# Squared-ReLU attention with a gated convolution: seven uneven query chunks a batch, or six of four tiles with the 25th tile's product turned round

## The chip, the cores and the metric

The kernel runs on one core of a Trainium2 chip. The metric is the device time of one execution in microseconds (us); three runs of the kernel before gave 2265.54 to 2267.61 us, median 2266.53. Engines are named as in the profile: PE is TensorE (matmuls) and PEld its loading of weights, DVE is VectorE, ACT is ScalarE, POOL is GpSimd, SP issues most DMAs.

## What is computed

```python
scores = scale * np.matmul(z, z.transpose(0, 2, 1))      # scale = 1/S; z is (8, 3200, 64)
attn = np.maximum(scores, 0.0) ** 2
x = u * np.matmul(attn, v)                                # u, v are (8, 3200, 256)
xp = np.concatenate([np.zeros((B, K - 1, D)), x], axis=1)
gate_pre += conv_w[k][None, None, :] * xp[:, k:k + S, :]  # for k in range(5)
gate = 1.0 / (1.0 + np.exp(-gate_pre))
out = (gate * (x @ w_val)) @ w_out                        # both weights are (256, 256)
```

Everything is float32. All products are made of three: each operand is split into a high part (float32r) and a low part (the rest), and high by high, high by low and low by high are added up in PSUM.

## The kernel before, in words

A batch has 3,200 positions, which are 25 tiles of 128. The queries of a batch are cut into seven chunks of 4, 4, 4, 4, 3, 3 and 3 tiles (the last batch: 4, 4, 4, 4, 4, 3, 2). For each chunk the keys are passed over in 13 steps, twelve pairs of tiles and the single last one, so a batch has 91 steps. In a step TensorE makes the scores of two key tiles against the chunk's queries (`scores`, into one of two PSUM bank pairs `s`), ScalarE applies ReLU and square (L581, L582) and casts the high part `ah` (L584), VectorE subtracts for the low part `al` (L590), and TensorE adds the product with v into the two banks `acc` (one for each half of the 256 features): v is stationary and the weights of the attention move, up to 512 columns wide. The scores are made three steps ahead of their product (`AHEAD`).

The matrix of scores is symmetric. A block that an earlier chunk has computed is transposed by VectorE (`turned`, L460 and L470), written to DRAM (`mir`) and later fetched (`m`), three steps ahead of its cast (`FETCH`); for such a step TensorE makes no scores.

Matmuls come in two forms. `side_by_side` (L386) splits the 128 rows of the contraction in two halves of 64 and issues matmuls of the two halves in turn, to two banks: a pair. Steps that have neither scores nor other work in them run as `attend_whole` (L634), 128 rows at once.

A chunk's conv stage runs beside the next chunk's steps, by the table `BEHIND`: x (u times attention, L664), its high and low part (L686, L691), five taps of the convolution for each half of the features (L703, L705), the sigmoid (L710), the product with `w_val` into the banks `misc`, its product with the gate (`gv`, L763, one for each of the two banks, at steps 6 to 9) and that one's high and low part (L767, L772). The product with `w_out` (`project`) goes into the same `misc` banks in the chunk after that, and its result through `ob` to DRAM. The order on each engine is the order in which the code issues the instructions: the loop over the steps issues TensorE's work of a step (attention products, scores, and what fills it), then what the table `todo` holds for the step, then the casts of the weights. Loads of z and v for the next batch, their transposes and their high and low parts have tables of their own (`Z_FROM`, `V_LOAD`, `V_HIGH`). At the end the last chunk's conv stage has nothing beside it; ten matmuls without use (`no_wait`, L393) stand in it.

In the code, `b` is the batch, `c` the chunk, `i` the pair of key tiles, `h` and `e` halves of the features, `P` is 128, `DH` is 2, `D` is 256, `CW` is 512 columns.

## Time and profile before

| what | value |
| --- | --- |
| time, median of three runs | 2266.53 us |
| span of the profiled execution | 2267.0 us |
| TensorE busy | 2259.1 us, 21,193 matmuls |
| VectorE busy | 1850.3 us, 2,421 instructions |
| ScalarE busy | 1746.5 us, 2,314 instructions |
| GpSimd busy | 67.8 us, 110 instructions |
| DMA | 380.73 MB, mean 168 GB/s |

The profile is of one execution, with a page of summaries and a trace behind it. In a group's row stand the line of the code, the engine, the operation, output and input, the shape and the count; then the busy time in us and the mean of one instruction in ns; then the idle time of the engine ahead of these instructions and whose work ended it. In the timeline a row has its start, its length, engine, line and operation. Matmuls are pipelined: the length of one is longer than the interval at which they start, so intervals are read from starts. A busy time of a group is the union of its matmuls' lengths.

### The profile page before, as it was taken

How to read it: one execution, taken by the hardware profiler on the slowest of the kernel's cores; microseconds unless marked ns; L12 is line 12 of the kernel's file. 1: busy time of each engine (PE TensorE's matmuls, PEld its weight loads, DVE VectorE, ACT ScalarE, POOL GpSimd, SP SyncE). 2: the span in 40 equal slices, each digit the busy share in tenths (PEclk: the TensorE clock that was granted, in tenths of full speed). 3: DMA queues.
4: the chain of work that ended last, by engine and by line, in shares of the span. 5: the costliest groups of instructions: out<-in, count | busy, mean ns of one | idle time of the engine just before them, and what ended most of it. 6: DMA issues, size and time to landing. Idle time of an engine off the chain costs nothing.

```text
span 2267.0 us, 52349 instructions
## 1 busy us (share of the span) xinstructions
PE 2259.1 (100%) x21193; PEld 1989.1 (88%) x21193; DVE 1850.3 (82%) x2421; ACT 1746.5 (77%) x2314; POOL 67.8 (3%) x110
## 2 busy tenths in 40 slices
PE   9999999999999999999999999999999999999999
PEld 7889988899888998889988899888998889988888
DVE  8887798877888779887888877888788887888776
ACT  8986799766987659877698776987769876697755
POOL 0000000000000000000000000000000000000000
PEclk9999999999999999999999999999999999999999
DMA  5555867779677786777877868778697776877753
GB/s 120 118 135 133 198 161 161 177 164 211 164 161 175 168 202 162 164 180 169 199 160 170 182 160 195 160 177 182 152 205 164 181 172 161 195 168 175 195 149 93
DMA packets 696547, 380.73 MB, mean 168 GB/s; under 512 B 399600, under 2 KB 666864, under 8 KB 696304
## 3 DMA queue, kind: packets, MB, share of 16 engines
q1 hardware_dynamic: 695104, 377.11, 71.7%
q8 instruction: 166, 2.72, 0.5%
q14 instruction: 77, 0.63, 0.1%
q10 hardware_dynamic: 1200, 0.26, 0.1%
HBM read 208.74 MB, written 168.49 MB: 166 GB/s over the span
## 4 chain that ended last, share of the span: by engine, by line
PE 99%; DVE 1%; issue 0%; ACT 0%; DVEq 0%
PE acc L386 68%; PE s L386 11%; PE misc L386 10%; PE acc L634 8%; PE misc L826 1%; PE misc L750 1%; PE misc L393 0%; DVE x L664 0%; DVE turned L470 0%; DVE v_hl L373 0%; DVE ah L586 0%; PE acc L826 0%; PE s L750 0%; DVE zhl L236 0%; DVE a L519 0%
## 5 line engine op out<-in xcount | busy, mean ns | idle before, releaser
L386 PE MATMUL acc<-ah,v_hl 64*128 64x512 f32 (+1 forms) x9800 | 1530.7, 369 | 1.8 <-DVE x L664 1.1
L386 PEld LDWEIGHTS acc<-ah,v_hl 64*128 64x128 f32 x9800 | 910.7, 184 | 135.2 <-DVE x L664 1.9
L386 PE MATMUL acc<-al,v_hl 64*128 64x512 f32 (+1 forms) x4900 | 911.5, 369 | 0.0
L590 DVE TENSOR_TENSOR al<-a,ah 128x1024 fp32r<-128x1024 f32 (+3 forms) x380 | 414.9, 1092 | 215.3 <-ACT ah L584 208.3
L386 PEld LDWEIGHTS acc<-al,v_hl 64*128 64x128 f32 x4900 | 459.4, 184 | 65.8 <-DVE al L508 0.9
L581 ACT ACTIVATE a<-s 128x1024 f32<-128x1024 f32 (+3 forms) x380 | 348.9, 918 | 169.8 <-PE s L386 158.7
L582 ACT ACTIVATE a<-a 128x1024 f32<-128x1024 f32 (+3 forms) x380 | 364.3, 959 | 12.1
L584 ACT CAST ah<-m 128x768 fp32r<-128x768 f32 (+2 forms) x309 | 275.0, 894 | 128.0 <-DMA m<-mir 53.1
L590 DVE TENSOR_TENSOR al<-m,ah 128x768 fp32r<-128x768 f32 (+2 forms) x309 | 314.8, 1020 | 40.5 <-ACT ah L584 38.9
L584 ACT CAST ah<-a 128x1024 fp32r<-128x1024 f32 (+3 forms) x345 | 328.6, 952 | 11.3
L460 DVE STREAM_TRANSPOSE turned<-a 128x1024 f32<-128x1024 f32 (+2 forms) x324 | 326.0, 1013 | 2.2 <-DMA mir<-turned 1.6
L705 DVE SCALAR_TENSOR_TENSOR gate<-x,cw,gate 128x512 f32<-128x512 f32 (+2 forms) x448 | 304.4, 679 | 4.4 <-ACT gate L703 0.3
L386 PE MATMUL s<-zq,zhl 64*128 64x512 f32 (+3 forms) x1722 | 230.2, 371 | 0.0
L386 PEld LDWEIGHTS s<-zq,zhl 64*128 64x128 f32 x1722 | 157.6, 184 | 26.1
L634 PE MATMUL acc<-ah,v_hl 128*128 128x384 f32 (+2 forms) x700 | 177.6, 331 | 0.2 <-DVE x L664 0.2
L664 DVE TENSOR_TENSOR x<-acc,ut 128x512 f32<-128x512 f32 (+2 forms) x112 | 65.8, 629 | 82.4 <-PE acc L386 53.4
L634 PEld LDWEIGHTS acc<-ah,v_hl 128*128 128x128 f32 x700 | 124.6, 188 | 4.7 <-issue 1.9
L634 PE MATMUL acc<-al,v_hl 128*128 128x384 f32 (+2 forms) x350 | 115.4, 330 | 0.0
L710 ACT ACTIVATE gate<-gate 128x512 f32<-128x512 f32 (+2 forms) x112 | 65.5, 585 | 60.6 <-DVE gate L705 60.4
L767 ACT CAST gvh<-gv 128x512 fp32r<-128x512 f32 (+2 forms) x112 | 64.0, 572 | 44.3 <-DVE gv L763 44.1
L763 DVE TENSOR_TENSOR gv<-misc,gate 128x512 f32<-128x512 f32 (+1 forms) x110 | 69.7, 633 | 17.2 <-PE misc L386 10.7
L703 ACT ACTIVATE gate<-x,cw 128x512 f32<-128x512 f32 (+2 forms) x111 | 75.0, 676 | 2.6 <-DVE x L664 2.6
(133 smaller groups left out, 1954.9 us busy)
## 6 DMA issues: line engine op xcount, KB each, us to landing
m<-mir SPq DMA_DIRECT2D x193, 384.0 KB, 5.1
mir<-turned SPq DMA_DIRECT2D x344, 192.0 KB, 3.3
mir<-turned SPq DMA_DIRECT2D x196, 256.0 KB, 4.0
m<-mir SPq DMA_DIRECT2D x98, 512.0 KB, 5.0
u_raw<-in_u_dram SPq DMA_DIRECT2D x264, 64.0 KB, 3.7
v_raw<-in_v_dram SPq DMA_DIRECT2D x116, 128.0 KB, 4.7
mir<-turned SPq DMA_DIRECT2D x84, 144.0 KB, 2.6
out_dram<-ob SPq DMA_DIRECT2D x92, 128.0 KB, 3.0
```

Of the source, the lines that this page charges most:

```text
L386: ins = nc.tensor.matmul(out_, st[r], mv[r], start=first, stop=last)
L460: nc.vector.transpose(into[:, t : t + m], a[:, j * w : (j + m) * w].rearrange("p (t m x) -> p t m x", t=m, x=BLK))
L581: nc.scalar.activation(a.rearrange("p (j x) -> p j x", j=2), s[:, :, :each], AF.Relu, scale=scale)
L582: nc.scalar.activation(a, a, AF.Square)
L584: nc.scalar.copy(hi, a)
L590: nc.vector.tensor_tensor(lo, a, f32(hi), op=ALU.subtract)
L634: nc.tensor.matmul(out_, st, mv, start=first, stop=last)
L664: nc.vector.tensor_tensor(x[:, h, HALO : HALO + w], accs[b, c][h][:, :w], ut[b, c][:, h, :w], op=ALU.mult)
L703: (first or nc.scalar.mul)(g, tap, cw[:, h, 0:1])
L705: nc.vector.scalar_tensor_tensor(g, tap, cw[:, h, k : k + 1], g, op0=ALU.mult, op1=ALU.add)
L710: nc.scalar.activation(g, g, AF.Sigmoid)
L763: nc.vector.tensor_tensor(gv[:, :w], pvs[b, c][e][:, :w], gates[b, c][:, e, :w], op=ALU.mult)
```

## The change

There are now six chunks of four tiles. The 25th tile of the queries has no chunk: its attention product is made in steps of the sixth chunk, written out as strings (`LAST_MIX`, `FIRST_MIX`): K is the step of the single key tile, whose scores for the 25th tile are made with those of the sixth chunk; O, F and C are the chunk's own, fetched and computed steps; each of three S steps takes eight key tiles of the 25th tile, whose scores were all computed by earlier chunks and are fetched. A batch has 81 steps.

In these products the attention weights are stationary (128 queries wide) and v moves: its two halves side by side, high and low part in 512 columns, then the high part in 256 (`swap_list`). The two halves of the rows go to the two banks of one of the two bank pairs `s`, which stays taken (`held_s`) until `one_take`: ScalarE copies one bank, VectorE adds the other to it and then the two halves of the result. In the meantime scores use the other bank pair alone.

The result has queries on the partitions, not features. The 25th tiles of two batches go together (`GROUPS`; the last two batches each alone): u is multiplied in by GpSimd, TensorE transposes (`one_turn`), and the group has a conv stage of its own (`one_place` to `one_out`), its steps counted from the start of the batch after the group: transposes at step 22 (the tenth step, numbered 9, of the second chunk, numbered 1), value product at 35 and 36, output product at 48 and 49.

Attention steps outside the last eight steps of the program are all pairs now. The loads of z and v and their parts have moved: those of z for the next batch start from the middle of the batch before on (`Z_FROM` counts from the next batch's start). The end of the program is new: after the last chunk's steps come the last 24 key tiles of the 25th tile's product, whole, and then the conv stages of the last chunk and of the last group; the ten matmuls without use are gone.

```diff
-    n_chunks = -(-NT // 4)
-    base, extra = divmod(NT, n_chunks)
-    even = [base + 1] * extra + [base] * (n_chunks - extra)
...
+    assert NT % 4 == 1
+    n_chunks = NT // 4
+    ONE = n_chunks
+    sizes = [4] * n_chunks + [1]
+    firsts = [4 * c for c in range(n_chunks + 1)]
...
+    LAST_MIX = {False: "KFOFFSFFFSFOSFFF", True: "FFOFFFFFOKFFFSSS"}
+    FIRST_MIX = "KCOFFSCFFSFOSFFF"
...
+    def s_bank():
+        if held_s[0] is None:
+            next_s[0] = 1 - next_s[0]
+            x = 1 - next_s[0]
+        else:
+            x = 1 - held_s[0]
+        return ps.tile([P, 2, 512], F32, name=f"s{x}", bufs=1)
...
+    def swap_list(b, c, i, bank):
+        if b not in swaps:
+            held_s[0] = next_s[0]
+            swaps[b] = ps.tile([P, 2, 512], F32, name=f"s{held_s[0]}", bufs=1)
+            swapped[b] = 0
+        out_ = swaps[b][:, bank]
+        if c == ONE:
+            k, n = tiles(c, i)
+            ah, al = (x[:, : n * P].rearrange("p (j x) -> p j x", j=n) for x in at[b, c, i])
+        else:
+            k, n, w = NT - 1, 1, sizes[c] * P
+            ah, al = (x[:, w : w + P].rearrange("p (j x) -> p j x", j=1) for x in at[b, c, i])
+        mms = []
+        for j in range(n):
+            both_v = vt[b, (k + j) // 2][:, :, (k + j) % 2]
+            first = swapped[b] + j == 0
+            last = swapped[b] + j == NT - 1
+            whole = (out_.rearrange("p (x d) -> p x d", x=2), ah[:, j], both_v, first, last)
+            half = (out_[:, :D], al[:, j], both_v[:, 0], False, False)
+            mms += [whole, half] if first else [half, whole]
+        return mms
+    def swap(b, c, i, piece=0, pieces=1):
+        sides = [swap_list(b, c, i, bank) for bank in range(2)]
+        side_by_side(*cut(sides, piece, pieces))
+        if piece == pieces - 1:
+            swapped[b] += tiles(c, i)[1]
...
+    GROUPS = ((0, 1), (2, 3), (4, 5), (6,), (7,))
...
+    def one_take(b, halves=True):
+        g, t = group_of(b)
+        if t == 0:
+            one_sum[g] = sb.tile([P, 2, D], F32, name="one_sum", bufs=1)
+        banks = swaps.pop(b)
+        part = sb.tile([P, CW], F32, name="gv", bufs=1)
+        if halves:
+            nc.scalar.copy(part, banks[:, 1])
+            nc.vector.tensor_tensor(part, banks[:, 0], part, op=ALU.add)
+            nc.vector.tensor_tensor(one_sum[g][:, t], part[:, :D], part[:, D:], op=ALU.add)
...
+        next_s[0] = held_s[0]
+        held_s[0] = None
...
+                for x in range(2):
+                    to = one_turned[g][x][:, (t * DH + h) * half : (t * DH + h + 1) * half]
+                    src = one_sum[g][rows[x], t, h * P : (h + 1) * P]
+                    nc.tensor.matmul(to, src, ident1[rows[x]], start=True, stop=True, is_transpose=True)
...
-    Z_FROM = {b: (-12, -7, -1, 7, 17, 23, 37) if b > 1 else (22, 26, 4, 8, 15, 30, 37) for b in range(1, B)}
-
-    U_LOAD = ((6, -1, -8, -11, -11, -11, -6), (-6, -2, -2, -9, -11, -11, -7))
-    U_PREP = ((11, 2, 1, 2) + (1,) * (n_chunks - 4), (10, 10, 3) + (1,) * (n_chunks - 3))
+    Z_FROM = {b: (-53, -48, -41, -33, -22, -10, -15) if b > 1 else (-17, -13, -35, -31, -24, -9, -5) for b in range(1, B)}
...
+    V_HIGH = (7, 8, 9, 10, 12, 13, 14, 15, 18, 19, 16, 17, 4)
...
+            if steps[s][1] == ONE and s < WHOLE_FROM:
+                for piece in range(2):
+                    fill_at(s + piece, swap, *steps[s], piece, 2)
+                done = s + 1
+            elif both(*steps[s][1:]) and s < WHOLE_FROM:
+                fill_at(s, swap, *steps[s])
+        if b < B - 1:
+            at_step(done, one_take, b)
...
+    for g, members in enumerate(GROUPS[:-1]):
+        s0 = start(members[-1] + 1, 0)
+        at_step(s0 + 6, one_load, g)
+        at_step(s0 + 9, one_mul, g)
+        fill_at(s0 + 22, one_turn, g)
+        at_step(s0 + 22, one_place, g)
+        at_step(s0 + 23, one_high, g)
+        at_step(s0 + 24, one_low, g)
+        for h in range(DH):
+            for k in range(KW):
+                at_step(s0 + 24 + 4 * h + max(k - 1, 0), one_conv, g, h, k)
+        at_step(s0 + 32, one_sigmoid, g)
+        for part in range(2):
+            fill_at(s0 + 35 + part, one_value, g, part)
+        for e in range(DH):
+            at_step(s0 + 36 + e, one_gated, g, e)
+        at_step(s0 + 37, one_gated_high, g)
+        at_step(s0 + 38, one_gated_low, g)
+        for part in range(2):
+            fill_at(s0 + 48 + part, one_project, g, part)
+        at_step(s0 + 49, one_out, g)
...
-            if not halved:
-                assert not left
-                if before:
-                    project_whole(*before)
-                for h in range(DH if 0 <= s < END else 0):
-                    attend_whole(b, c, i, h)
...
+            if s >= WHOLE_FROM:
+                assert not left and not terms and not piece and not before
+                if s < END:
+                    for h in range(DH):
+                        attend_whole(b, c, i, h)
+                    if both(c, i):
+                        swap_whole(b, c, i)
...
+        for h in range(DH):
+            attend_whole(*steps[END], h)
+        project_whole(b, c - 1)
...
+        for s in range(END + 1, N):
+            swap_whole(*steps[s])
+        for x in range(DH):
+            out_copy(b, c - 1, x)
+        out_store(b, c - 1)
+        for k in range(1, KW):
+            conv(b, c, 1, k)
+        sigmoid(b, c, one[0])
+        sigmoid(b, c, one[1])
+        one_take(b, False)
+        one_mul(g, nc.vector)
...
         for e in range(DH):
             value_whole(b, c, e, spare=True)
-        no_wait(*warm, 10)
+        one_turn(g)
+        one_place(g)
...
+        for h in range(DH):
+            for k in range(KW):
+                one_conv(g, h, k)
+        one_sigmoid(g)
+        project_whole(b, c, spare=True)
+        for part in range(2):
+            one_value(g, part)
+        for e in range(DH):
+            one_gated(g, e)
+        one_gated_high(g)
+        one_gated_low(g)
         for x in range(DH):
-            out_copy(b, c - 1, x)
-        out_store(b, c - 1)
-        project_whole(b, c, spare=True)
-        for x, tag in enumerate(("zz", "z_raw")):
-            ob = sb.tile([P, CW // P * D // 2], F32, name="ob_half", tag=tag, bufs=1)[:, : all_sizes[b][c] * D // 2]
-            (nc.scalar.copy, nc.vector.tensor_copy)[x](
-                ob.rearrange("p (i x c) -> p x i c", x=DH, c=BLK),
-                pos[b, c][x][:, : all_sizes[b][c] * D // 2].rearrange("p (x i c) -> p x i c", x=DH, c=BLK),
-            )
-            f = all_firsts[b][c]
-            (nc.scalar, nc.sync)[x].dma_start(
-                out[b, f * P :, :].rearrange("(t x p) d -> x p t d", p=P, x=DH)[x],
-                ob.rearrange("p (t d) -> p t d", d=D),
-            )
+            out_copy(b, c, x)
+        out_store(b, c)
+        for part in range(2):
+            one_project(g, part)
+        one_out(g)
```

On TensorE, in chunk 1 of the third batch (b = 2), these rows stand around the scores of step 9 before; `s`, `acc` and `misc` are PSUM banks, and a row with x6 is six matmuls:

```order
L386 MATMUL acc_9430<-ah,v_hl_8841 128x512
L386 MATMUL acc_9429<-ah,v_hl_8841 128x512
L386 MATMUL s<-zhl_7019 128x256 x6
L386 MATMUL acc_9429<-ah,v_hl_8841 128x512
L386 MATMUL acc_9430<-ah,v_hl_8841 128x512
```

And in the changed kernel at the same place:

```order
L419 MATMUL acc_8852<-ah,v_hl_8201 128x512
L419 MATMUL acc_8853<-ah,v_hl_8201 128x512
L419 MATMUL s_9317<-zhl_6085 128x256 x6
L1047 MATMUL misc_9324<-ident_75,one_sum 128x64
L1047 MATMUL misc_9325<-ident_75,one_sum 128x64
```

The group's transposes (eight in all) have been put between the scores and the attention product that follows.

On VectorE, in chunk 2 of the same batch, these are the rows that lead up to the second `gv` before; `al` is the low part of attention weights, `gate` a tap of the convolution:

```order
L590 TENSOR_TENSOR al<-m,ah 128x4x2x128
L705 SCALAR_TENSOR_TENSOR gate<-x,cw,gate 128x512 x2
L590 TENSOR_TENSOR al<-a,ah 128x1024
L460 STREAM_TRANSPOSE turned<-a 128x2x16x32
L705 SCALAR_TENSOR_TENSOR gate<-x,cw,gate 128x512 x2
L590 TENSOR_TENSOR al<-m,ah 128x4x2x128
L763 TENSOR_TENSOR gv<-misc_10318,gate 128x512
L705 SCALAR_TENSOR_TENSOR gate<-x,cw,gate 128x512
```

And in the changed kernel:

```order
L640 TENSOR_TENSOR al<-m,ah 128x4x2x128
L797 SCALAR_TENSOR_TENSOR gate<-x,cw,gate 128x512 x2
L1092 SCALAR_TENSOR_TENSOR one_sum<-one_f,cw,one_sum 128x256
L640 TENSOR_TENSOR al<-a,ah 128x1024
L511 STREAM_TRANSPOSE turned<-a 128x2x16x32
L797 SCALAR_TENSOR_TENSOR gate<-x,cw,gate 128x512 x2
L215 STREAM_TRANSPOSE zz<-z_raw 128x4x4x32
L1092 SCALAR_TENSOR_TENSOR one_sum<-one_f,cw,one_sum 128x256
L640 TENSOR_TENSOR al<-m,ah 128x4x2x128
L855 TENSOR_TENSOR gv<-misc_9774,gate 128x512
```

Taps of the group's convolution (L1092) and a transpose of z (L215) have come in between; five more taps stand further up in the chunk and the low part of z further down, ahead of the second `gv`.

On VectorE at the end of the second batch of the changed kernel, around the taking of the held bank (L1011, L1012):

```order
L406 TENSOR_TENSOR v_hl_7872<-v_raw,v_hl_7872 128x512
L640 TENSOR_TENSOR al<-m,ah 128x4x2x128 x2
L1011 TENSOR_TENSOR gv<-s_7385,gv 128x512
L1012 TENSOR_TENSOR one_sum<-gv 128x256
L406 TENSOR_TENSOR v_hl_7938<-v_raw,v_hl_7938 128x512
L636 CAST ah<-a 128x1024
```

Before there is no such step; the low parts of v (L406, there L373) and of the attention weights stand at the end of a batch there too.

More of the change, by code (lines that the diff above doesn't have):

```diff
@@ L241, in has_copy @@
     def has_copy(b, c, i=None):
-        if i is not None and place[b, c, i] >= NP - 2 and c < n_chunks - 1 and spread(b, c + 1):
+        if i is not None and place[b, c, i] >= NP - 2 and has_copy(b, c + 1):
             return False
@@ L260, in attn_glu_kernel, with tiles, own @@
     NP = len(pairs)
+    GROUP = 8
+    def tiles(c, i):
+        return (GROUP * i, GROUP) if c == ONE else pairs[i]
     def two_pairs(b, c):
-        first = all_firsts[b][c]
-        return all_sizes[b][c] == 4 and first % 2 == 0 and first < NT // 2 + 2 and (b > 0 or c > 1)
-    def own(b, c, x):
-        return all_firsts[b][c] // 2 + x
+        return c < n_chunks and (b > 0 or c > 1)
+    def own(c, x):
+        return 2 * c + x
+    SINGLE = NP - 1
     MIRRORED_AT = {
@@ L295, in attn_glu_kernel @@
             if two_pairs(b, c):
-                order.append(order.pop(own(b, c, 1)))
-            if spread(b, c):
-                fetched = [i for i in order if mirrored(b, c, i)]
-                computed = [i for i in order if not mirrored(b, c, i)]
-                at_ = MIRRORED_AT[len(fetched)]
-                order = [(fetched if p in at_ else computed).pop(0) for p in range(NP)]
-            if b == B - 1 and c == n_chunks - 1:
-                new = [i for i in order if sum(pairs[i]) > all_firsts[b][c]]
-                order = new + [i for i in order if i not in new]
@@ new lines, in attn_glu_kernel, with start, position @@
+            starts[b, c] = len(steps)
+            for p, (x, i) in enumerate(order):
+                place[b, x, i] = p
+                steps.append((b, x, i))
+    N = len(steps)
+    def start(b, c):
+        c = min(c, n_chunks - 1)
+        return starts[b, c] if b < B else N
+    def position(s):
+        b, c, _ = steps[s]
+        c = min(c, n_chunks - 1)
+        return b, c, s - starts[b, c]
+    ends_main = {}
+    for s, (b, c, _) in enumerate(steps):
+        if c < n_chunks:
+            ends_main.setdefault((b, c), [s, s])[1] = s
@@ new lines, in attn_glu_kernel, with one_turn @@
+    one_turned = {}
+    def one_turn(g):
+        n = len(GROUPS[g])
+        half = P // 2
+        one_turned[g] = [ps.tile([P, 512], F32, name=f"misc{x}", bufs=1) for x in range(2)]
+        for t in range(n):
+            for h in range(DH):
[3 more added lines that the diff above has]
+                    nc.tensor.matmul(to, src, ident1[rows[x]], start=True, stop=True, is_transpose=True)
@@ new lines, in one_gated_low, with one_project_list @@
+    def one_gated_low(g, engine=nc.vector):
+        w = len(GROUPS[g]) * P
+        engine.tensor_tensor(one_r[g][:, 2:, :w], one_gate(g), f32(one_r[g][:, :2, :w]), op=ALU.subtract)
+    def one_project_list(g, x, banks, first, last):
+        n = len(GROUPS[g])
+        wh, wl = weights["out"]
+        gvh, gvl = (one_r[g][:, 2 * y : 2 * y + 2] for y in range(2))
+        places = [(x, e) for e in range(DH)] if n == 2 else [(0, x)]
+        out_ = []
+        for p, (t, e) in enumerate(places):
+            ts = slice(t * P, (t + 1) * P)
+            for m, (gp, wp) in enumerate(((gvl, wh), (gvh, wl), (gvh, wh))):
+                ends = p == len(places) - 1 and m == 2
+                out_.append((banks[x][:, :D], gp[:, e, ts], wp[:, e], first and p == m == 0, last and ends))
+        return out_
@@ L933, in value_places @@
             return ()
-        return VALUE_AT.get(sum(mirrored(b, c, i) for i in range(NP)), ())
+        if c == n_chunks - 1:
+            return (4, 7)
+        return (4, 5, 6) if sum(mirrored(b, c, i) for i in range(NP)) == 8 else ()
     def project_places(b, c):
@@ L1152, in attn_glu_kernel @@
                     fn(*args)
-                if s >= 0 and not whole:
+                if s >= 0 and not whole and c != ONE:
                     left.append((b, c, i))
-                if terms or fill or behind:
+                if terms or fill or behind or s + 1 == WHOLE_FROM:
                     for n in range(len(left)):
```

529 lines of the change are left out of this document (319 added, 210 removed), and 2 rows, old and new, of the table MIRRORED_AT.

## Prediction

> **What bounds the kernel now.** I read the first and the fourth part of the page, then TensorE's groups by form, then the timeline at the places that the change touches.
>
> ```profile
> PE 2259.1 (100%) x21193; PEld 1989.1 (88%) x21193; DVE 1850.3 (82%) x2421; ACT 1746.5 (77%) x2314; POOL 67.8 (3%) x110
> PE 99%; DVE 1%; issue 0%; ACT 0%; DVEq 0%
> ```
>
> TensorE is busy for 2259.1 of 2267.0 us and makes up 99% of the chain that ended last. So the time is the sum of the intervals at which matmuls start, plus the few places where TensorE waits. VectorE at 82% and ScalarE at 77% have room on average, but not at every place.
>
> ```profile
> L386 PE MATMUL acc<-ah,v_hl 64*128 64x512 f32 x6528 | 1079.7, 387 | 1.8 <-DVE x L664 1.1 <-DVE ah L521 0.5
> L386 PE MATMUL acc<-ah,v_hl 64*128 64x384 f32 x3272 | 451.0, 333 | 0.0
> L634 PE MATMUL acc<-ah,v_hl 128*128 128x384 f32 x564 | 147.3, 336 | 0.0
> ```
>
> These are the largest groups: attention products on four tiles of queries (512 columns) and on three (384), as side-by-side pairs (64 rows each) or whole (128 rows). The mean ns of one is its latency and not what it costs. The cost is the interval between starts, from the timeline:
>
> ```profile
> 1002.67 0.39 PE L386 MATMUL acc<-al,v_hl 64*128 64x512 f32 x2
> 1003.35 0.39 PE L386 MATMUL acc<-al,v_hl 64*128 64x512 f32 x2
> ...
> 1097.74 0.34 PE L386 MATMUL acc<-ah,v_hl 64*128 64x384 f32 x2
> 1097.91 0.33 PE L386 MATMUL acc<-al,v_hl 64*128 64x384 f32 x2
> 1098.09 0.34 PE L386 MATMUL acc<-ah,v_hl 64*128 64x384 f32 x2
> 1098.35 0.44 PE L634 MATMUL acc<-ah,v_hl 128*128 128x384 f32 x1
> ...
> 1117.43 0.33 PE L634 MATMUL acc<-al,v_hl 128*128 128x384 f32 x1
> 1120.20 0.33 PE L750 MATMUL misc<-xh,w_val_hi 128*128 128x384 f32 x1
> ...
> 2256.00 0.28 PE L826 MATMUL misc<-w_out_hi,gvl 128*128 128x256 f32 x1
> 2258.04 0.28 PE L826 MATMUL misc<-w_out_hi,gvh 128*128 128x256 f32 x1
> ```
>
> Three pairs of 512 lie between the first two rows: 0.68 us, 0.227 a pair. Between the rows of 1117.43 and 1120.20 lie 16 whole matmuls of 384: 0.173 each, and the 384 pairs of 1097.74 to 1098.09 have about the same interval. Between the last two lie 17 whole ones of 256: 0.120 each. From the last pair of 384 to the first whole one it is 0.26 instead of 0.17: a switch between the two forms costs about 0.09.
>
> **TensorE's work.** I multiply the counts of both programs by these intervals (0.227 for 512, 0.173 for 384, 0.117 for a pair of 256, which the rows at 939.39 below give, 0.120 whole). For pairs of 192, 128 and 64 columns I take 0.10 as an estimate, below the 0.117 of 256; there are few of them. The terms:
> - Attention products: before 4,896 pairs of 512, 2,454 pairs of 384, and 846 of 384, 54 of 512 and 150 of 256 whole, 1711.1 us. After, 7,122 pairs of 512 and 78 whole, 1632.3; to this come the products of the 25th tile with v moving, 175 pairs of 512, 175 pairs of 256 and 25 of each whole, 68.8. Together −10.0. Three tiles at 0.173 are 0.0577 a tile, four at 0.227 are 0.0567.
> - Value products: 138.1 to 130.6, −7.5. Output products: 138.9 to 132.9, −6.0 (whole ones of 256 become fewer). Scores: 243.2 to 239.3, −3.9. Most of these three is the 25th tile's own conv stage leaving the chunks.
> - That stage for the groups: 32 transposes, 24 pairs of 128 and 84 of 256 columns, +15.6.
>
> The sum is 2237.6 to 2225.7: −11.9 us.
>
> TensorE's start of 1.5 us and its last end at 2263.0 leave 2261.5 us, so 23.9 us lie between the clean sum and what it took. Part of it goes with the change: the three-tile chunks (23 of 56) and the switches between pairs and whole matmuls, some two per batch. The switches alone are 2 us. If the 23 chunks carry their share and a little less than all the rest, it is 15. I take 8.5 (0.37 a chunk), an estimate between these ends.
>
> **The new waits on TensorE.** The groups' steps use the misc banks, which the conv stage of the chunk before still holds until VectorE has read the second one (gv, the second of two). In the orders these steps stand right behind the scores of the ninth step. In chunk 1:
>
> ```profile
> 939.39 0.52 PE L386 MATMUL s<-zhl 64*128 64x256 f32 x6
> 939.74 0.40 PE L386 MATMUL acc<-ah,v_hl 64*128 64x512 f32 x2
> 940.32 0.69 DVE L763 TENSOR_TENSOR gv<-misc,gate 128x512 f32<-128x512 f32 x1
> ```
>
> Scores end their turn at 939.74 (three pairs in 0.35, the 0.117 above). The bank is free at 941.01. The transposes that now stand at 939.74 would wait 1.3 us, with the scores, pairs and everything else on TensorE queued behind them: four groups, +5.2 us. Nothing waits today, since the next matmul writes another bank.
>
> In chunk 2 it is the group's value product:
>
> ```profile
> 984.13 0.69 DVE L763 TENSOR_TENSOR gv<-misc,gate 128x512 f32<-128x512 f32 x1
> 984.36 0.52 PE L386 MATMUL s<-zhl 64*128 64x256 f32 x6
> 984.71 0.40 PE L386 MATMUL acc<-ah,v_hl 64*128 64x512 f32 x2
> ...
> 957.23 1.22 DVE L590 TENSOR_TENSOR al<-a,ah 128x1024 fp32r<-128x1024 f32 x1 [1.13 <-ACT ah L584]
> 964.33 1.23 DVE L590 TENSOR_TENSOR al<-a,ah 128x1024 fp32r<-128x1024 f32 x1 [0.59 <-ACT ah L584]
> 979.28 1.23 DVE L590 TENSOR_TENSOR al<-a,ah 128x1024 fp32r<-128x1024 f32 x1 [2.06 <-ACT ah L584]
> ...
> L705 DVE SCALAR_TENSOR_TENSOR gate<-x,cw,gate 128x256 f32<-128x256 f32 x8 | 3.9, 484 | 0.5 <-ACT gate L703 0.3
> L219 DVE STREAM_TRANSPOSE zz<-z_raw 128x512 f32<-128x512 f32 x31 | 21.8, 704 | 3.5 <-DMA z_raw<-in_z_dram 3.4
> L236 DVE TENSOR_TENSOR zhl<-zz,zhl 128x512 fp32r<-128x512 f32 x31 | 21.2, 684 | 0.7 <-ACT zhl L231 0.7
> L231 ACT CAST zhl<-zz 128x512 fp32r<-128x512 f32 x30 | 18.7, 622 | 9.5 <-DVE zz L219 9.3
> L710 ACT ACTIVATE gate<-gate 128x512 f32<-128x512 f32 x66 | 41.7, 631 | 47.1 <-DVE gate L705 47.1
> ```
>
> Before, the bank is free at 984.82, 0.1 after TensorE passes. After, VectorE has seven taps of the group's conv (0.484 each, by the row of 256 columns), a transpose of z (0.70) and its low part (0.68) ahead of that gv: 4.8 us. It had 1.13, 0.59 and 2.06 us of idle time in that stretch, 3.8 in all, so it comes 1.0 us later. All three idle times are waits for ScalarE's ah, and ScalarE gets a sigmoid (0.63) and a cast of z (0.62) in the same stretch: if these stand ahead of the ah that VectorE waits for, it is 1.0 + 1.25 = 2.25 later. I take this end, since the sigmoid stands behind VectorE's last tap and so holds ScalarE's queue. With the 0.1, 2.3 us for three groups of two; for the group of one tile, with taps half as wide, 0.4. Together +7.3, bounds 1 to 8. If VectorE had been idle enough, this would be 0.
>
> In chunk 3 the group's output product is at the same step:
>
> ```profile
> 1025.74 0.69 DVE L763 TENSOR_TENSOR gv<-misc,gate 128x512 f32<-128x512 f32 x1
> 1026.81 0.62 PE L386 MATMUL acc<-ah,v_hl 64*128 64x512 f32 x4
> ```
>
> gv ends at 1026.43 and TensorE reaches the place at about 1027: nothing, with 0.5 us to spare.
>
> **The handover of the score bank.** The 25th tile's sum holds one of two score banks until ScalarE has copied half of it and VectorE has added it; the first scores after that write this bank. In the order 12 pairs of 512 lie between the last product and those scores: 2.72 us. The copy and the add by their nearest rows:
>
> ```profile
> L581 ACT ACTIVATE a<-s 128x512 f32<-128x512 f32 x34 | 20.1, 590 | 25.6 <-PE s L386 25.6
> L664 DVE TENSOR_TENSOR x<-acc,ut 128x512 f32<-128x512 f32 x66 | 42.5, 687 | 58.8 <-PE acc L386 48.7 <-issue 9.5 <-PE acc L634 0.5
> ```
>
> 0.59 + 0.69 = 1.3 with nothing ahead of them, so 1.4 us of cover: cost 0, if neither engine is more than 1.4 us behind.
>
> **The tail.** After the last attention product TensorE had 11.0 us to the end of the span:
>
> ```profile
> 2255.88 0.28 PE L634 MATMUL acc<-ah,v_hl 128*128 128x256 f32 x1
> 2263.05 0.42 DVE L1217 COPY ob_half<-acc 128x256 f32<-128x256 f32 x1 [0.70 <-PE acc L826]
> 2263.50 0.66 SPq L1222 DMA_DIRECT2D out_dram<-ob_half  x1
> ```
>
> Of these, 52 matmuls of 256 at 0.12 are 6.2 us of TensorE work, and 4.8 are not. Now the last tile's conv stage is a chain of its own behind its last product: 12 value products (2.7), transposes (0.4), two copies (0.7), the two casts of gv that stand in the same queue (1.2), high and low part (0.8), two low parts of gv (1.3), eight taps (3.0), sigmoid (0.4), value product (0.7), gating and its high and low part (1.4), output product (0.7), copies (0.8) and the same 3.5 us from the last VectorE instruction to the end: 17.6. These are estimates from rows of the same operations, 128 columns taken at 0.37. TensorE's own work in it is 7.4 (with the last chunk's 24 output products), so 10.2 are not. That is +5.4 us, bounds 3 to 8.
>
> **The sum.** −11.9 − 8.5 + 5.2 + 7.3 + 0 + 5.4 = −2.5 us on the span of 2267.0: 2264.5. The median of the runs, 2266.53, is 0.5 below the profiled span, so 2264.0.
>
> **The rivals.**
> 1. *The groups' waits are hidden.* VectorE and ScalarE are about 2 us earlier in chunks 1 and 2 than I think, because attention steps that were whole are now pairs and the tables for z and v have moved. Speaks for it: the 3.8 us of VectorE's idle time above. Against: the 1.3 us in chunk 1 is read straight from the trace, where VectorE isn't idle. Then 12.5 us less: 2251.5.
> 2. *TensorE waits for the score bank at the handover (the slower side).* In the sixth chunk v of the next batch is split too, and each step casts or subtracts 1,024 columns, of 1.0 to 1.2 us. One such instruction ahead of the copy and one ahead of the add use up the 1.4 us; two on each cost 1.0 + 1.2 + 1.3 + 1.0 − 2.7 = 1.8 us. With seven batches that is 12.3 us: 2276.3. It decides from 1.4 us of delay on.
> 3. *The clock falls in the tail.* TensorE pauses for about 3.5 us while the eight taps run, and the ten filler matmuls that stood in the old tail are gone. The trace shows what a slow clock costs, at the start:
>
> ```profile
> L393 PE MATMUL misc<-zeros 128*128 128x512 f32 x13 | 5.4, 592 | 1.5 <-DVE zeros L1085 1.5
> ```
>
> There 512 columns take 5.4/13 = 0.415 us instead of 0.227. With the last products at that rate, 3 us more: 2267.0. The Trainium skill, page "TensorE: Matmul & The Clock Gate", section "Part 1: The HAM clock gate (the "warmup" mystery)", says that the clock is halved after an idle window of some 3.4 us; by it this rival would happen if the pause fills such a window, and no run here shows it, since the trace of before has no such pause.
>
> **How the numbers follow.** The sum as it stands 0.50, with some ±6 us of its own from the bounds of the waits and of the 8.5; rival 1 0.25, rival 2 0.20, rival 3 0.05. A measurement of this kernel tells 0.2% from no change, 4.5 us: faster is below 2262.0, slower above 2271.1. Of the sum's 0.50, 0.15 lie below, 0.30 within, 0.05 above; of rival 1, 0.24 below; of rival 2, 0.19 above; rival 3 lies within. So faster 0.39, same 0.37, slower 0.24. The range takes in the greater part of rivals 1 and 2, with a fifth of all cases outside: 2250 to 2277.
>
> **What would show it.** Right: TensorE idle 1 to 2.5 us ahead of the groups' transposes and value products, released by VectorE's gv; no idle time ahead of the first scores after the handover; attention products at 0.227 throughout; 17 to 18 us behind the last product of the 25th tile. Wrong: no idle time at the groups' steps (rival 1), idle time ahead of those scores released by VectorE's add (rival 2), a granted clock below 1 at the end (rival 3), or a product with v moving whose pairs start more than 0.227 and 0.117 apart, since the trace of before has none: at 10% more it would be 7 us.

## The result, and the profile after

The changed kernel takes 2281.78 us (median of four runs, 2280.77 to 2283.24) against 2266.8 for the kernel before: a ratio of 1.0062, 95% interval 1.0048 to 1.0076. It is slower by 14 us (15 by the two medians), where 2264.0 was forecast with a range of 2250 to 2277. The profiled execution has a span of 2280.4 us, 13.4 more than before.

The first lines of the page, as before:

```profile
PE 2255.2 (99%) x20597; PEld 1966.7 (86%) x20597; DVE 1836.4 (81%) x2249; ACT 1720.2 (75%) x2187; POOL 77.8 (3%) x114
PE 86%; DVE 5%; ACT 4%; issue 2%; DMA 1%; SPq 1%; DVEq 0%; ACTq 0%
```

TensorE has less to do (2255.2 us busy instead of 2259.1, in a longer span), but the chain that ended last now runs through VectorE, ScalarE and DMA for 11% of the span, with 2% of issue beside it, where VectorE had 1%. TensorE's waits, with the total, the number and the longest:

```profile
PE misc L419 <- DVE gv L855: 5.6, 3, 1.9
PE misc L1047 <- DVE gv L855: 4.4, 4, 1.1
PE acc L918 <- DVE gvl L864: 3.1, 1, 3.1
PE acc L419 <- DVE al L640: 2.0, 7, 0.8
PE misc L419 <- DVE one_r L1127: 1.6, 1, 1.6
...
PE acc L419 <- ACT ah L634: 1.1, 1, 1.1
PE s L842 <- DVE one_sum L1015: 1.0, 1, 1.0
```

The first two are the waits at the groups' value products (three times) and transposes (four times). No scores (`s`) wait for the taking of the held bank (L1011, L1012), so the handover costs nothing in the seven batches that it was forecast for; the last line is the last batch's, in the tail. Here is the group's transpose in chunk 1, the place of the rows at 939 to 941 us before:

```profile
1216.81 0.40 PE L419 MATMUL s<-zhl 64*128 64x256 f32 x4
1217.05 0.22 PE L1047 MATMUL misc<-ident,one_sum 64*128 64x64 f32 x1
1217.62 0.69 DVE L855 TENSOR_TENSOR gv<-misc,gate 128x512 f32<-128x512 f32 x1
1218.36 0.40 PE L1047 MATMUL misc<-ident,one_sum 64*128 64x64 f32 x6 [1.10 <-DVE gv L855]
```

One transpose finds its bank free; the other bank is free when `gv` ends at 1218.3. From start to start that is 1.3 us.

Adding the intervals between the starts of successive matmuls over both traces, by kind, shows where the time went. An interval counts for the matmul that it begins with; the value products of before include the ten matmuls without use (1.7 us).

| kind | before | after | difference | forecast, work alone |
| --- | --- | --- | --- | --- |
| attention products, the 25th tile's included | 1725.8 | 1722.2 | −3.6 | −10.0 |
| scores | 246.6 | 243.2 | −3.4 | −3.9 |
| value products | 139.6 | 130.9 | −8.7 | −7.5 |
| output products | 142.3 | 140.2 | −2.1 | −6.0 |
| groups' and last tile's own stage | 0 | 32.1 | +32.1 | +15.6 |

The work is as counted. What was added to it isn't: the groups' own stage takes twice its matmuls, and the attention products give back two thirds of their gain. In the trace these are, beside the 11.8 us at the groups (5.2 and 6.6 by intervals): 2.8 us behind the value products (three times 0.42 by intervals, some 25 us behind, where VectorE's `al` comes late, and once 1.5 of a slow clock); one stall of the first batch at 236 us, 4.2 us with what surrounds it, 1.4 of them a slow clock; a wait of 0.20 us in the fifth chunk of six batches, 0.49 by intervals, 2.9 in all; and the tail. Behind the last product of the 25th tile, which starts at 2257.94 and takes its 0.23 us, the tail has 22.2 us to the end of the span, where 17.6 were forecast.

The slow clock is a loss of its own. TensorE's granted clock fell to 0.50 in the main loop twice, from 237.34 to 240.75 behind the stall, and from 704.97 to 708.38 behind the first of the three waits of 1.86 us at the value products. In this trace the clock changes only on a grid of 3.413 us (see the last section). Four stretches of that grid follow (from and to, length, TensorE's busy time and matmuls, granted clock): the first wait lies in one stretch, the second, of the same length, is cut by a border. Below them are two rows of the slow stretch:

```profile
701.56:704.97 3.41, 1.55 (x23) 1.00 0.99 227
704.97:708.38 3.41, 3.41 (x20) 0.50 0.85 245
1261.34:1264.75 3.41, 2.60 (x27) 1.00 0.88 160
1264.75:1268.17 3.42, 2.37 (x26) 1.00 0.84 207
...
706.21 1.26 PE L419 MATMUL acc<-ah,v_hl 64*128 64x512 f32 x4
707.06 0.83 PE L419 MATMUL acc<-al,v_hl 64*128 64x512 f32 x2
```

Two pairs of 512 take 0.85 us there instead of 0.45. Which wait is followed by a slow stretch differs from one execution to the next, and some of the differences between the runs below are no more than that.

The stall of the first batch, on ScalarE, VectorE and TensorE:

```profile
234.91 1.04 ACT L634 CAST ah<-m 128x1024 fp32r<-128x1024 f32 x1 [7.90 <-DMA m<-mir]
235.99 1.22 DVE L640 TENSOR_TENSOR al<-m,ah 128x1024 fp32r<-128x1024 f32 x1 [7.25 <-ACT ah L634]
236.01 0.50 PE L419 MATMUL acc<-ah,v_hl 64*128 64x512 f32 x2 [1.09 <-ACT ah L634]
237.26 0.75 PE L419 MATMUL acc<-al,v_hl 64*128 64x512 f32 x2 [0.76 <-DVE al L640]
```

A fetched block arrives late, and all three engines stand. SP's queue shows why:

```profile
210.28 0.43 SPq L542 DMA_DIRECT2D m<-mir  x1
219.07 3.42 SPq L990 DMA_DIRECT2D out_dram<-ob  x4
222.54 1.29 SPq L161 DMA_DIRECT2D u_raw<-in_u_dram  x2
223.88 2.09 SPq L161 DMA_DIRECT2D z_raw<-in_z_dram  x4
226.01 3.02 SPq L533 DMA_DIRECT2D mir<-turned  x4
229.13 1.13 SPq L546 DMA_DIRECT2D m<-mir  x1
```

The queue stood for 8 us at the store of results (`ob` wasn't ready), and the block waited behind that, a load of u, the load of z that the change has put there and a store of turned blocks. The kernel before has that standstill too (6.0 us, to 214.17), but with no load of z between it and the fetch, and TensorE didn't wait.

The tail by stretches; the figure behind the five engines' busy times is the granted clock (PEclk):

```profile
2246.00:2258.00 12.00, 12.00 (x77) 10.76 (x75) 9.55 (x14) 4.11 (x9) 0.59 (x1) 1.00 0.13 44
2262.00:2266.00 4.00, 0.87 (x7) 0.47 (x6) 2.63 (x5) 2.55 (x7) 0.00 (x0) 0.86 0.00 0
2266.00:2271.00 5.00, 5.00 (x24) 4.93 (x24) 2.92 (x9) 0.42 (x1) 0.00 (x0) 0.50 0.00 0
```

TensorE has 0.9 of 4 us of work from 2262 to 2266, and then a clock of 0.50 while it makes the last chunk's output product. Two rows of that product, seven matmuls apart:

```profile
2266.33 0.41 PE L918 MATMUL acc<-w_out_hi,gvh 128*128 128x256 f32 x1
...
2267.82 0.41 PE L918 MATMUL acc<-w_out_hi,gvl 128*128 128x256 f32 x1
```

0.213 us each, instead of 0.120.

### The profile page after: what moved, and what is told of

Same layout as the page of the kernel before. It is cut to its first block, busy times and chain, and to the rows that moved or that the text cites. A ratio compares the mean times of both kernels' runs of the same rounds, so it can differ in the third digit from the quotient of the medians.

```text
span 2280.4 us, 50544 instructions
## 1 busy us (share of the span) xinstructions
PE 2255.2 (99%) x20597; PEld 1966.7 (86%) x20597; DVE 1836.4 (81%) x2249; ACT 1720.2 (75%) x2187; POOL 77.8 (3%) x114
## 4 chain that ended last, share of the span: by engine, by line
PE 86%; DVE 5%; ACT 4%; issue 2%; DMA 1%; SPq 1%; DVEq 0%; ACTq 0%
PE acc L419 62%; PE s L419 12%; PE misc L419 10%; DVE al L640 2%; ACT ah L634 1%; ACT a L632 1%; ACT a L631 1%; DMA m<-mir 1%; DVE turned L511 1%; PE acc L721 1%; DVE ut L740 1%; DVE gate L797 0%; DMA mir<-turned 0%; PE s L704 0%; DVE xl L783 0%
## 5 line engine op out<-in xcount | busy, mean ns | idle before, releaser
L419 PE MATMUL acc<-ah,v_hl 64*128 64x512 f32 x9496 | 1622.2, 388 | 1.6 <-ACT ah L634 1.1
L419 PE MATMUL acc<-al,v_hl 64*128 64x512 f32 x4748 | 979.4, 388 | 2.1 <-DVE al L640 2.0
L640 DVE TENSOR_TENSOR al<-a,ah 128x1024 fp32r<-128x1024 f32 (+1 forms) x346 | 399.7, 1155 | 197.9 <-ACT ah L634 196.2
L631 ACT ACTIVATE a<-s 128x1024 f32<-128x1024 f32 (+1 forms) x346 | 333.5, 964 | 144.9 <-PE s L419 143.5
L632 ACT ACTIVATE a<-a 128x1024 f32<-128x1024 f32 (+1 forms) x346 | 347.6, 1005 | 11.0
L634 ACT CAST ah<-m 128x1024 fp32r<-128x1024 f32 x254 | 264.7, 1049 | 113.6 <-PE acc L419 75.0
L640 DVE TENSOR_TENSOR al<-m,ah 128x1024 fp32r<-128x1024 f32 x254 | 308.1, 1213 | 50.6 <-ACT ah L634 50.6
L634 ACT CAST ah<-a 128x1024 fp32r<-128x1024 f32 (+1 forms) x323 | 319.9, 990 | 10.3
L511 DVE STREAM_TRANSPOSE turned<-a 128x1024 f32<-128x1024 f32 (+1 forms) x278 | 318.4, 1145 | 0.0
L797 DVE SCALAR_TENSOR_TENSOR gate<-x,cw,gate 128x512 f32<-128x512 f32 x384 | 283.4, 738 | 3.6
L855 DVE TENSOR_TENSOR gv<-misc,gate 128x512 f32<-128x512 f32 x94 | 64.5, 686 | 21.9 <-PE misc L419 17.6
```

What stands on the lines that cost most here:

```text
L419: ins = nc.tensor.matmul(out_, st[r], mv[r], start=first, stop=last)
L511: nc.vector.transpose(into[:, t : t + m], a[:, j * w : (j + m) * w].rearrange("p (t m x) -> p t m x", t=m, x=BLK))
L631: nc.scalar.activation(a[:, : n * w].rearrange("p (j x) -> p j x", j=2), s[:, :, :each], AF.Relu, scale=scale)
L632: nc.scalar.activation(a, a, AF.Square)
L634: nc.scalar.copy(hi, a)
L640: nc.vector.tensor_tensor(lo, a, f32(hi), op=ALU.subtract)
```

## The experiments

All ratios are to runs of the kernel before on the same chip; the changed kernel stands at 1.0062 (1.0048 to 1.0076). Where an edit is worth 2 to 5 us the two intervals overlap, and the reading rests on the run's trace.

**Every step of the groups one later.**

```diff
-        fill_at(s0 + 22, one_turn, g)
+        fill_at(s0 + 23, one_turn, g)
...
-            fill_at(s0 + 35 + part, one_value, g, part)
+            fill_at(s0 + 36 + part, one_value, g, part)
...
-            at_step(s0 + 36 + e, one_gated, g, e)
+            at_step(s0 + 37 + e, one_gated, g, e)
```

> Every step of the groups' conv stages from the transposes on comes one step later (transposes in step 10 instead of 9 of the second chunk, value product in steps 10 and 11 of the third, output product in 10 and 11 of the fourth); nothing else is changed. Theory A (the trace of the changed kernel): TensorE waits 1.3 us ahead of the transposes four times and 2.1 us ahead of the value products three times, with some 2.7 us of shorter waits behind them, only because VectorE has not yet read the misc bank; a step is 5.4 us of TensorE's work, so all of it goes: 2281.8 - 14 = 2268, at least 2271. Theory B: VectorE is itself the bound in these stretches, so the wait turns up at the next place that needs it: 2278 to 2282.

Measured 1.0076 (1.0063 to 1.0088): nothing gained. The two waits are gone, and this one is there:

```profile
PE misc L419 <- DVE one_sum L1119: 12.5, 4, 3.3
```

It is the output product of an ordinary chunk, in step 1 of the next chunk, which now waits for the group's gating (L1119) to leave the misc banks: four times 3.3 us at most. Behind two of them the clock fell as well (715.19 to 718.60 and 1274.97 to 1281.80), 4.2 us more. The size is at least theory B's, but the place points to a cause that neither theory has, since the edit had moved the gating too. So the next run keeps the gating where it was.

**The groups' products later, the gating in place.**

```diff
-        fill_at(s0 + 22, one_turn, g)
-        at_step(s0 + 22, one_place, g)
+        fill_at(s0 + 23, one_turn, g)
+        at_step(s0 + 23, one_place, g)
...
-            fill_at(s0 + 35 + part, one_value, g, part)
+            fill_at(s0 + 36, one_value, g, part)
```

> The group's transposes come one step later and both halves of its value product stand in the step that had the second half (step 10 of the second and of the third chunk); all the rest of the groups' stage keeps its step, the gating that frees the misc banks for the next chunk above all. Theory A (the waits are at the misc banks, and in the run with every step shifted they only moved to the next chunk's output product, 12.5 us, because the gating was shifted too): the 5.2 us at the transposes and 6.6 us at the value products go and nothing comes in their place, 11 to 13 us less than the changed kernel, a ratio of 1.000 to 1.002 to the kernel before. Theory B (VectorE is the bound in these two chunks and its lag must turn up somewhere): the ratio stays at 1.005 to 1.007 and TensorE waits at the next chunk's output product again.

Measured 1.0021 (1.0013 to 1.0030), 9 us less than the changed kernel: theory A, a little short. No wait at the misc banks is left; in their place TensorE waits some 3 us more for VectorE's `al`:

```profile
PE acc L419 <- DVE al L640: 5.1, 10, 1.1
```

Three of these waits, of 1.0 to 1.1 us, stand some 22 us behind the value products, in the next chunk. So a part of the lag, about a quarter of the 11.8 us, does turn up again, and the rest was the order.

**The groups left out.** The conv stages of the first four groups aren't issued; the rows of the 25th tiles of seven batches are not computed beyond their attention product.

> The changed kernel without the conv stages of the first four groups: the rows of the 25th tiles of the first seven batches are not computed further than their attention product and not stored. Theory A (the groups cost their matmuls, 15.6 x 7/8 = 13.7 us, and the waits that the trace shows at them and right behind them, 5.2 + 6.6 + 2.8 = 14.6): 28 us less than the changed kernel, a ratio of 0.993 to 0.995. Theory B (much of these waits is a lag of VectorE that shows elsewhere without them): 0.997 to 1.000.

Measured 0.9936 (0.9923 to 0.9948), 28.6 us less than the changed kernel. That is theory A's size. The first batch's stall, which the groups don't touch, takes 1.6 us in this run's trace instead of 4.2, so some 26 us are the groups' own, about half of it work and half waits.

**A filler in the tail.**

```diff
         one_turn(g)
+        no_wait(*warm, 24)
         one_place(g)
```

> 24 matmuls of 256 columns without use stand in the 3.1 us pause of TensorE between the last group's transposes and the last chunk's output product; nothing else is changed. Theory A (the clock fell in the tail): the output product's 24 matmuls go back from 0.213 to 0.120 us each, its end comes 2.2 us earlier, and the group's value product then waits for the sigmoid instead, which ends 1.5 us ahead of where that product starts now: 2281.8 - 1.5 = 2280.3, at most 2.5 us gained, with a granted clock back at 1.00. Theory B (VectorE's chain of taps sets the end, whatever the clock): 2281.8, no change.

Measured 1.0049 (1.0036 to 1.0062). From the start of the last chunk's value product to the end of the span it is 18.8 us (2256.83 to 2275.6) instead of 21.1 (2259.31 to 2280.4): 2.3 us gained there. The stretch of the output product, and two of its rows, seven apart:

```profile
2262.00:2266.00 4.00, 3.84 (x32) 3.67 (x32) 3.65 (x10) 0.73 (x3) 0.00 (x0) 1.00 0.00 0
...
2263.53 0.28 PE L918 MATMUL acc<-w_out_lo,gvh 128*128 128x256 f32 x1
2264.37 0.28 PE L918 MATMUL acc<-w_out_hi,gvh 128*128 128x256 f32 x1
```

Clock 1.00 and 0.120 us each: theory A.

**The filler, and the last tile's value product ahead of the last chunk's output product.**

```diff
+        for part in range(2):
+            one_value(g, part)
         project_whole(b, c, spare=True)
-        for part in range(2):
-            one_value(g, part)
```

> The tail alone: 24 matmuls without use after the last group's transposes, as before, and the group's value product ahead of the last chunk's output product instead of behind it. Theory A (the last group's gating waits for its value product, which waits for the slow output product): the gating starts at the sigmoid's end, 3.7 us earlier than in the changed kernel, and the end with it: 3.5 to 5.5 us less than the changed kernel, a ratio of 1.004 to 1.005. Theory B (ScalarE's copies of the last chunk's results and their store set the end): as with the filler alone, 1.005 or more.

Measured 1.0043 (1.0030 to 1.0055). From the value product to the end it is 16.8 us (2257.21 to 2274.0), 4.3 less than the changed kernel and 2.0 less than with the filler alone. Theory A.

**The first batch's fetch.** Two runs. The first moved the wrong block (the sixth chunk's first, which stands behind the late one on the queue):

```diff
+                early = 3 if (steps[s][:2], s - start(0, 5)) == ((0, 5), 3) else 0
+                at_step(s - AHEAD - FETCH - early, m_fetch, *steps[s], first=True)
```

> The first block that the sixth chunk of the first batch fetches is issued three steps earlier on SP's queue, ahead of the store of results that SP waits for; nothing else is changed. Theory A (the 2.3 us stall at 236 us and the 1.9 us of shorter ones around it come from SP's queue alone): 2281.8 - 4 = 2278. Theory B (ScalarE and VectorE are behind there anyway, or the next block is late in its turn): 2281 to 2282.

Measured 1.0059 (1.0045 to 1.0073), no change; the late block went out together with the one that was moved up and came at 235.7 us. TensorE's two waits there grew to 2.96 us (1.85 in the changed kernel), but the clock didn't fall behind them; it fell at 704 and 1267 us instead. One of the five executions took 2276.09 us, with a mean granted clock of 0.999; the others took 2281.83 to 2284.32, with 0.996 or 0.997. The second moves the late block itself, the last that the fifth chunk fetches:

```diff
+                early = 2 if s == starts[0, 4] + 12 else 0
+                at_step(s - AHEAD - FETCH - early, m_fetch, *steps[s], first=True)
```

> The changed kernel with one edit: in the first batch the last block that the fifth chunk fetches is issued two steps earlier, so that it stands ahead of the store of results, of a load of z and of a store of a turned block on SP's queue (the run with an earlier fetch had moved another block). Theory A (that block landing at 235 us is the whole of the stall there): the waits of 232 to 244 us go, 4.2 us in the changed kernel's trace and 2 to 4 in the other runs: a ratio of 1.0045 to 1.0055 against 1.0062. Theory B (the next block of that queue is late then): 1.006 to 1.007.

Measured 1.0049 (1.0037 to 1.0062), 3 us less: in theory A's range, with an interval that reaches into theory B's. The trace decides for A: between 232 and 244 us TensorE doesn't wait at all. Of the 4.2 us, 1.4 were the slow clock, which not every execution has there.

**The fourth chunk's z earlier.**

```diff
-    Z_FROM = {b: (-53, -48, -41, -33, -22, -10, -15) if b > 1 else (-17, -13, -35, -31, -24, -9, -5) for b in range(1, B)}
+    Z_FROM = {b: (-53, -48, -41, -36, -22, -10, -15) if b > 1 else (-17, -13, -35, -31, -24, -9, -5) for b in range(1, B)}
```

> The load of the fourth chunk's z for the next batch, with its transpose and its parts, comes three steps earlier (step -36 instead of -33 from the next batch's start), so that its low part no longer stands ahead of a subtraction of the fifth chunk's third step; nothing else is changed. Theory A (this low part of 0.65 us on VectorE makes the 0.36 us wait and its 0.48 us in all, once a batch): six batches, 2281.8 - 2.9 = 2279. Theory B (the wait comes from ScalarE's two casts of fetched blocks standing behind its copy of results): 2281 to 2282.

Measured 1.0040 (1.0027 to 1.0053), 5 us less than the changed kernel; the six waits are gone. That is 2 us more than theory A said. In this run's profile the first batch's stall was shorter too (0.53 us instead of 1.09 of waiting for `ah`), though the edit doesn't touch that batch, and the clock didn't fall in the main loop, where the two falls of the changed kernel cost 2.9 us. Within the run the time goes with the mean granted clock as well: 2275.57 us at 0.999, 2279.84 at 0.996. So the edit itself is worth theory A's 2.9, and the rest need not be its doing.

**All mends, and two more.** The second edit of the groups, the tail with its two edits, the fetch and the z.

> The changed kernel with four mends at once: the groups' steps as in the first run of this call, the tail as in the third, the fourth chunk's z three steps earlier, and in the first batch the fifth chunk's last fetched block issued two steps earlier, ahead of the store of results on SP's queue. Theory A (the waits add up and are independent): 12 + 4.5 + 3 + 2 = 21 us less than the changed kernel, 6 us less than the kernel before, a ratio of 0.996 to 0.998. Theory B (they share VectorE's lag, and one gives back what the other gains): 0.999 to 1.003.

Measured 0.9983 (0.9974 to 0.9992), 18 us less than the changed kernel and 4 less than the kernel before: the version that beats both, by 0.17%. It is between the two theories and nearer to A: somewhat less than the mends add up to (21). What is left:

```profile
PE acc L419 <- DVE al L640: 3.1, 3, 1.1
PE misc L426 <- DVE zeros L1353: 1.5, 1, 1.5
PE s L842 <- DVE one_sum L1015: 1.0, 1, 1.0
```

Two more edits were to take the first and the third of these:

```diff
-    Z_FROM = {b: (-53, -48, -41, -36, -22, -10, -15) if b > 1 else (-17, -13, -35, -31, -24, -9, -5) for b in range(1, B)}
+    Z_FROM = {b: (-47, -43, -39, -35, -22, -10, -15) if b > 1 else (-17, -13, -35, -31, -24, -9, -5) for b in range(1, B)}
...
+        next_s[0] = 1 - next_s[0]
```

> All mends, and two more: the last chunk's value product goes to the score bank that the 25th tile's sum didn't use, and the loads of the first four chunks' z of the next batch come 6, 5, 2 and 1 steps later, so that their transposes and low parts stand behind the group's taps. Theory A (what is left of waits in the run with all mends is 1.0 us at the last chunk's value product and three times 1.3 us behind the group's value product, where VectorE is behind by the z work): 4 to 5 us less than with the first mends, a ratio of 0.996 to 0.997. Theory B (VectorE's lag there comes from the taps and the gating alone): 0.998.

Measured 0.9993 (0.9984 to 1.0002), 2 us worse than without them, though the intervals overlap. The third line is gone, but the first has become this:

```profile
PE acc L419 <- DVE al L640: 5.3, 4, 1.6
```

Theory A falls. Theory B, that the taps and the gating alone make the lag, isn't shown either: in the trace of all mends VectorE stands idle for 1.66 us at 1272.78, waiting for ScalarE's `ah`, so it has caught up with the group's work by then. What stands ahead of the late `al` (1279.61) is the work of the chunk itself, in one row: a turned block, x's low part, a transpose for `ob` and one of u. What makes this wait stays open.

**The kernel before with pairs for whole matmuls.** One part of the change alone:

```diff
-            halved = by_halves(s) or (by_halves(s - 1) and by_halves(s + 1))
+            halved = by_halves(s) or (by_halves(s - 1) and by_halves(s + 1)) or b < B - 1
...
-                if terms or fill or behind:
+                if terms or fill or behind or p == NP - 1 or len(left) > 1:
```

> The kernel before with one part of the change alone: in all batches but the last, every attention step runs as pairs, none as whole matmuls of 128 rows, and with them the output and value products that stood in such steps. Theory A (what TensorE takes beyond the clean intervals is not tied to the switch between whole matmuls and pairs, some 2 us in all): the ratio to the kernel before is 0.998 to 1.002. Theory B (the forecast's term: whole stretches and their switches carry a good part of 8.5 us): 0.996 to 0.998.

Measured 1.0037 (1.0024 to 1.0049), outside both. The trace shows why the run doesn't answer its question. In a step without scores, the two halves of a product now follow each other directly:

```profile
541.50 0.33 PE L386 MATMUL acc<-al,v_hl 64*128 64x384 f32 x2
541.67 0.84 PE L386 MATMUL acc<-ah,v_hl 64*128 64x384 f32 x4
542.35 0.34 PE L386 MATMUL acc<-al,v_hl 64*128 64x384 f32 x2
```

The two pairs of the middle row take 0.68 us from start to start instead of 0.35. Between them the halves of the rows change banks, and `turn_round` makes TensorE wait until the other half's matmuls have left them. That happens 30 times in attention products and 6 times in output products: 0.33 each, 12 us, and it doesn't occur in the main loop of the changed kernel, which puts the second halves behind scores or other work. Without these 12 us the run would be some 3.5 us faster than before, at the border between the two theories; that last step is worked out, not measured, and the question stays open.

## Why the prediction was wrong

The step that failed is the sum, "−11.9 − 8.5 + 5.2 + 7.3 + 0 + 5.4 = −2.5": the waits that were in its list came at nearly the right size, but the list was too short, and the tail was too small. It put at nothing all waits outside the groups' steps and the handover, and the clock that falls behind a wait. Term by term:

- *The work, −11.9*: right. Scores, value products and the groups' matmuls came as counted, and the run without groups agrees with the half that is work.
- *The new waits, +5.2 and +7.3*: 5.2 and 6.6 by intervals. The first price, read from the rows of before (a free bank at 941.01), held by its mechanism. The second held to 10%, partly by luck: the seven taps went into VectorE's idle time, of which 2.0 us were left in that stretch (1.55 of them at 1259.59, for ScalarE's `ah`). What came late was that `ah`: ScalarE did the cast of z and the group's sigmoid first and began the step's ReLU 2.30 us behind its scores, at 1256.37, where it had been 0.88. Behind it VectorE had z's low part (0.6) more. Missing were the 2.8 us behind the value products, 1.5 of them the slow clock.
- *The handover, 0*: right; in five other runs scores wait there once, in the first batch, for 0.3 to 0.7 us. Rival 2, which had the slower side with 12 us, is refuted: the kernel is slower without it.
- *The tail, +5.4*: mis-sized by 4.6 us. The clock fell, as rival 3 had it for 3 us and a chance of 0.05: 2.3 us by the run with the filler. It fell for another reason than was thought: not while the taps ran, when TensorE made the output product, but in the 3.1 us before, when the low parts were made. The order then cost 2.0 more, since the last tile's value product stood behind that output product. The Trainium skill, page "TensorE: Matmul & The Clock Gate", section "Part 1: The HAM clock gate (the "warmup" mystery)", has the clock halved after an idle window of some 3.4 us. By that page the chance should have been above 0.05, since the prediction itself had a pause of 3.5 us. The trace shows stretches of 3.41 us, but not that one must be idle throughout: 1.85 us of idle time was enough at 701.56. So the clock could fall in the main loop too, where the prediction had no rival for it: 1.4 and 1.5 us.
- *The excess over clean intervals, −8.5*: partly. What went: in the trace of before the 2,454 pairs of 384 take 430.7 us, 6.2 above 0.173 each, and the whole ones 1.8. What the step left out is that their work comes back in a form with an excess of its own: the 25th tile's 175 steps of a pair of 256 and one of 512 take 61.2 us instead of 60.2 clean, and a pair of 512 takes 0.2280 in the trace of before, 1.3 ns above clean, for 2,226 more pairs. A gross gain was entered as a net one. With the measured terms, −11.9 + 5.2 + 6.6 + 10.0 (the tail), and the 2.8 + 4.2 + 2.9 us of waits that weren't listed, the sum is +19.8; the span grew by 13.4, so some −6.4 is left for this term.
- *Not in the list at all*: SP's queue in the first batch (4.2 us in the profiled run, 3 by the run that moved the late block) and the low part of z in the fifth chunk (2.9 by the trace, and its run agrees). Moved loads of z have a part in both, which the prediction weighed on VectorE in chunk 2 alone; that the load of z alone makes the late fetch, beside the 8 us for the store of results, isn't shown. A load that moves has four instructions on SP's queue, a transpose, a cast and a subtraction, and each has new neighbours at each new place.

The chances went wrong with the list: waits unseen can only make the kernel slower, so the sum as it stood was the fast end of what it covered, and not its middle.

## What to carry to other kernels

A stage that is taken out of the main loop pays for its own waits at shared banks: price each at the place where it is put, then ask what frees the bank for the next user, because moving a step without its release moved 12 us of waiting and took none away. For every load that moves, go through each queue and engine that it touches, at its new place, in each batch that differs. A wait of TensorE may cost more than its length: look for a lower granted clock behind it. A gain from shapes that disappear is net only after the shapes that take over have been given the same excess.

## What the runs showed of the hardware

- TensorE's granted clock changes on a fixed grid. In the changed kernel's trace, behind the start, it changes at 237.34, 240.75, 704.97, 708.38, 2264.86, 2271.68 and 2275.10 us: all distances are multiples of 3.413 us (240.75 to 704.97 is 136 of them, 708.38 to 2264.86 is 456).
- In the main loops of all traces together, the clock went to 0.50 behind each stretch of this grid that held 1.84 us or more of idle time of TensorE (nine times), and behind none that held 1.82 or less. So it hangs on where a wait lies on the grid whether it costs another 1.4 to 1.6 us, which is what a single stretch at 0.50 took there.
- In the tail the clock fell behind less. In the changed kernel it was 0.50 behind a pause of 3.1 us, and whole products of 256 columns took 0.213 us instead of 0.120. In the run with the filler it fell again at 2269.30, behind a stretch with 1.15 us of idle time:

```profile
2267.83 0.39 PE L419 MATMUL misc<-one_r,w_val_hi 64*128 64x128 f32 x4
2269.84 0.58 PE L419 MATMUL misc<-w_out_hi,one_r 64*128 64x256 f32 x2 [1.63 <-DVE one_r L1127]
2270.22 0.42 PE L419 MATMUL misc<-w_out_lo,one_r 64*128 64x256 f32 x2
2270.43 1.06 PE L419 MATMUL misc<-w_out_hi,one_r 64*128 64x256 f32 x4
```

  Pairs of 256 start 0.21 us apart there, and 0.38 after the first. The matmuls just before were small ones (64 rows, 128 columns); whether that counts, no run here tests.
- Two halves of the rows that change banks without other work between them cost 0.33 us, with the wait that `turn_round` puts there.
- A fetch with another one right behind it landed later, in the one case that the runs have: the late block of the first batch took 5.8 us from its issue at 229.13 until ScalarE started on it, and 7.0 from 228.77 with a second fetch issued behind it.
